# A gated mix of attention and expert lookup: the loads of the output stage in another order, all from SyncE

## The chip, the cores and the metric

The kernel runs on one core of a Trainium2 chip. Its time is the device time in microseconds. A profile is one execution taken by the hardware profiler: it has its own device time, and a span, which runs from the first instruction to the last. The engines are TensorE (PE in the profile, with PEld for its weight loads), VectorE (DVE), ScalarE (ACT), GpSimd (POOL) and SyncE (SP). Each works through its own instructions in order. A transfer is issued by SP, ACT or POOL and carried by 16 DMA engines that all of them share. The profile names the hardware queue of SP q1, that of ACT q10 and that of POOL q0.

## What is computed

Two branches share the input x of 2048 tokens by 1024 features, and a gate per token mixes them:

```python
g = _sigmoid((x * gate_w).sum(-1, keepdims=True))
a = _A_ref(x, A_wqkv, A_wo)      # 32 heads of 32, softmax attention, then @ wo
b = _B_ref(x, B_w_q, B_k1, B_k2, B_u, B_v)   # per token and head, one of 64 experts
return g * a + (1 - g) * b
```

Everything is float32. The attention branch ends in a product of the heads' outputs, 2048 x 1024, with `wo`, 1024 x 1024. The expert branch ends in a product of a 2048 x 64 matrix of weights with `v`. The output stage of the kernel makes both of these last products.

## The kernel before

The program has four parts: the projections with the routing of experts, the values, the attention over 32 heads, and the output stage. The change touches the last head of attention and the output stage, which begins at about 1644 us of the profile.

**What attention leaves in memory.** Each head writes its unnormalized output to `OD[g]` (od in the profile; `finish`, line 1378), where g is one of 8 groups of 4 heads, and its row sums to `SMD[g]` (smd; `norm_sums`, line 1385). When a group of four heads is done, `load_r` (line 1393) reads the four sums back (rr<-smd), and `norm_r` (line 1397) takes reciprocals on VectorE, multiplies by the gate, and stores them in `RD` (rd<-rr).

**Blocks.** The output stage works on 8 blocks of 256 tokens. For block n it needs the rows of all groups, `OC[n]` (tile V; `load_o`, line 1406: 8 loads of 128 KB, one per group), and the reciprocals spread over the 32 features of every head, `RB[n]` (tile rb for block 0, accd for the others; `load_rb`, line 1412: 4 loads of 256 KB for 8 groups, each of which reads the same rows of `RD` into 32 partitions). `load_chunk` (line 1419) calls both. The tiles V and accd have two buffers each, so that block n + 2 takes the place of block n.

**Precision.** Each operand is split into a high and a low part: ScalarE makes the high part by a copy, and VectorE the low part by a subtraction (`split`, line 93). A product is three products of parts.

**Blocks 0 and 1** are computed plainly: `split_o` (line 1589) scales the rows by the reciprocals and splits them, `wo_mm` (line 1517) multiplies by the split `wo` (woh and wol), `av_mm` (line 1527) adds the expert branch, and `plain_out` (line 1581) copies the four PSUM banks to the tile `post` (the memory of rb) and stores them (out<-rb). Block 0 and block 1 use the same four places of `post`, so that the copies of block 1 wait for the stores of block 0 to land:

```python
            nc.scalar.activation(post[:, i], ps, AF.Copy)
        else:
            nc.vector.tensor_copy(post[:, i], ps)
        store(n, j, half, post[:, i])
```

**Blocks 2 to 7** use seven products in place of eight (`unit`, line 1662, with `Halves`, which builds the sums of operands). Four products need combined weights T1 to T4, which the values part wrote to memory as TD, and which `load_t` (line 1561) loads: t0h and t0l into wo_raw for P5, t1h and t1l into wo_raw for P6, t2h and t2l into z and t3l for P7, t3h and t3l into halves of woh and wol for P4. Each is 1 MB. `scale_o` (line 1572) scales a block's rows on VectorE. In `unit(2)`, after product P1, stand in this order: the copies and stores of block 1 (`plain_out`), the operands S4 and A22, and the operands of block 3, whose first step is `scale_o(3)`; only then come the sums of P1, P6, P7 and P5 on VectorE that set their PSUM banks free. The banks go round: eight of them, four for block 0, four for block 1, then one for each product. P2 of `unit(2)` takes the bank that the first copy of block 1 sets free, and P7 of `unit(3)` needs a bank that those sums set free.

**What sets the order.** The program is written out in the order in which each engine works. During attention a table of steps (`at`, line 1445) says after which step of which head a load is issued; from the output stage on, the order of the calls is the order of the queues. SP issues each transfer when its buffer is free, and also waits then for the transfer eight places earlier to have landed, since the completion semaphores go round in eights.

Of the kernel before, what the change touches and what calls it, by code (L numbers as in the profile page):

```python
# [10 lines left out]
F32R = mybir.dt.float32r  # L11
# [7 lines left out]
H = 32  # L19
KC = D // 128  # L20
HC = KC // 2
NT = S // 128
NQ = S // 512
G = H // 4
W = 256
# [6 lines left out]
def gated_mha_peer_kernel(ctx, tc, xT, wqkv, wv, wo, wq, k12, ug, v, out):  # L32
# [8 lines left out]
    nc = tc.nc  # L41
# [32 lines left out]
    def dma(dst, src, queue=nc.sync):  # L74
        a, b = (ap.bitcast(F32) if ap.dtype == F32R else ap for ap in (dst, src))
        return queue.dma_start(a, b)  # L76
# [16 lines left out]
    def split(hi, lo, src, on=None):  # L93
        nc.scalar.activation(hi, src, AF.Copy)  # L94
        (on or nc.vector).tensor_tensor(out=lo, in0=src, in1=hi.bitcast(F32), op=OP.subtract)
# [13 lines left out]
    def bank():  # L109
        i = bank_no[0] % 8  # L110
        bank_no[0] += 1
        return ps1.tile([128, 512], F32, name=f"bk{i}")
# [788 lines left out]
    zp = Pool("zp", side="right")  # L901
# [357 lines left out]
    wk = Pool("wk", bufs=2)  # L1259
# [88 lines left out]
    def rowsum(ps, *srcs):  # L1348
        for src in srcs:
            for qc in range(NQ):  # L1350
                yield nc.tensor.matmul(ps[32 * qc:32 * qc + 32, :], ones,  # L1351
                                       src[:, qc * 512:(qc + 1) * 512],
                                       start=(src is srcs[0]), stop=(src is srcs[-1]))
# [52 lines left out]
    def load_o(n, k0, k1, queue=nc.sync):  # L1406
        if k0 == 0:
            OC[n] = vpool.tile([128, KC, W], F32, name="V")
        for kc in range(k0, k1):
            dma(OC[n][:, kc, :], OD[kc][:, n * W:(n + 1) * W], queue)  # L1410

    def load_rb(n, k0, k1, js=range(4), queue=nc.sync):
        if k0 == 0 and js[0] == 0:
            RB[n] = rb0 if n == 0 else wk.tile([128, KC, W], F32, name="accd")
        for j in js:
            src = RD[k0:k1, j:j + 1, n * W:(n + 1) * W].rearrange("g j s -> j g s")
            dma(RB[n][32 * j:32 * j + 32, k0:k1, :], src.to_broadcast([32, k1 - k0, W]), queue)
# [7 lines left out]
    OH, OL, W0 = {}, {}, []  # L1425
# [19 lines left out]
    def at(step, f, *a):  # L1445
        todo.setdefault(step, []).append((f, a))
# [25 lines left out]
    at(30 * NT + 13, load_rb, 0, 0, KC - 1, range(2))  # L1472
    at((H - 1) * NT + 2, load_rb, 0, 0, KC - 1, range(2, 4))
    at((H - 1) * NT + 8, load_rb, 1, 0, KC - 1)
    at((H - 1) * NT + 14, load_rb, 2, 0, KC - 1)


    BT = 2
# [34 lines left out]
    def load_at(n):  # L1513
        AT[n] = fin.tile([128, W], F32R, name="at", bufs=3)
        dma(AT[n], ATD[:, n * W:(n + 1) * W])
# [45 lines left out]
    def load_t(i, *parts):  # L1561

        ops = ht.b.setdefault(f"T{i + 1}", [None, None])
        for n, (part, src) in enumerate(zip(parts, TD[i])):
            if part is None:
                continue
            m = HC // len(part)
            for j, place in enumerate(part):
                dma(place, src[:, m * j:m * j + m, :].rearrange("p k m -> p (k m)"))
            ops[n] = [place[:, k * 512:(k + 1) * 512] for place in part for k in range(m)]  # L1570
# [18 lines left out]
    def split_o(n, k0, k1):  # L1589
        o = OC[n][:, k0:k1, :]  # L1590
        nc.vector.tensor_mul(o, o, RB[n][:, k0:k1, :])
        split(OH[n][:, k0:k1, :], OL[n][:, k0:k1, :], o)

    def banks4():
        return {(i, half): bank() for i in range(W // 128) for half in range(2)}
# [4 lines left out]
    finish(H - 1)  # L1600
    sm = pso.tile([128, 512], F32, name="o")
    list(rowsum(sm, *(P[H - 1, NT - i] for i in (1, 2)), ACC.pop(H - 1)))
    load_o(1, 0, KC - 1, nc.gpsimd)
    split_hi(1)
    for kc in range(1, KC - 1):
        split_hi(kc + 1)
        if kc == 1:
            norm_sums(H - 1, sm, nc.scalar)
            load_r(G - 1)
            for n in range(2):  # L1610
                load_at(n)
            pso.close()
        split_lo(kc)
        wo_mm(pa, 0, [kc], False, False)
    norm_r(G - 1)
    for n in range(2):
        load_chunk(n, KC - 1, KC)
    load_rb(2, KC - 1, KC)
    split_lo(KC - 1)
    split(woh[0], wol[0], raw_wo(0))  # L1620

    load_t(2, None, [fin.tile([128, S], F32R, name="t3l")])
    load_t(0, *([keep.tile([128, S], F32R, name=f"wo_raw{j}")] for j in range(2)))
    ps_odd = Pool("ps_odd", space=PSUM)
    for (i, half), ps in pa.items():
        av_mm(0, i, half, ps)
    split_o(0, KC - 1, KC)
    wo_mm(pa, 0, [KC - 1], False, True)  # L1630
    OH[1] = zp.tile([128, KC, W], F32R, name="z1")
    OL[1] = wk.tile([128, KC, W], F32R, name="acc")
    for k0, k1 in ((0, HC), (HC, KC)):
        split_o(1, k0, k1)
    load_o(2, 0, KC)
    load_at(2)
    load_t(2, [zp.tile([128, S], F32R, name="z0")], None)
    load_t(1, *([keep.tile([128, S], F32R, name=f"wo_raw{2 + j}")] for j in range(2)))
    pa1 = banks4()
    wo_mm(pa1, 1, list(range(KC - 1)), True, False)  # L1640
    for (i, half), ps in pa1.items():
        av_mm(1, i, half, ps)
    plain_out(0, pa)
    load_t(3, *([part[k][:, 512:] for k in range(HC)] for part in (woh, wol)))
    load_rb(3, 0, KC, queue=nc.scalar)
    load_o(3, 0, KC)
    ht.places(wk.tile([128, S], F32R, name="acc"), "A11", "A12")
    ht.places(fin.tile([128, S], F32R, name="s31"), "S3", "S1")
    scale_o(2)
# [121 lines left out]
```

## Time and profile before

| | us |
|---|---|
| median of three runs | 1827.84 |
| the three runs | 1827.28, 1827.84, 1831.94 |
| the profiled execution's own time | 1832.25 |
| its span | 1830.4 |
| what lies around the span | 1.85 |
| PE busy in the span | 1817.8 |

The page of the profile gives the busy time of each engine and the costliest groups of instructions. Below it, the trace answers questions about single instructions: a timeline of one engine, in which a bracket at the end of a row tells how long the engine had been idle and what ended that; busy time, granted TensorE clock and DMA rate in chosen stretches; and the chain of work that ended last. Matmul rows are pipelined: of two rows that follow one another, the second's start counts, not the first's end.

### The profile page before, as it was taken

The numbers are of one execution on the slowest core, as the hardware profiler recorded it, in microseconds if no ns is written. First come the engines' busy times: TensorE is split into PE (matmuls) and PEld (weight loads), VectorE is DVE, ScalarE is ACT, GpSimd is POOL, SyncE is SP. The second block draws the span as 40 slices with busy tenths as digits, with TensorE's granted clock in tenths as the row PEclk, the third lists the DMA queues.
The fourth block names the chain that finished last, engine by engine and source line by source line (L and its number), as shares of the span: only waits on it lengthen the run. The fifth ranks groups of instructions, "written<-read, shape, count | busy, mean of one in ns | idle before, by whom it ended". The sixth has DMA issues, their size and how long they took to land.

```text
span 1830.4 us, 26559 instructions
## 1 busy us (share of the span) xinstructions
PE 1817.8 (99%) x10083; PEld 1099.8 (60%) x10083; DVE 1461.4 (80%) x1258; ACT 1312.5 (72%) x1716; POOL 231.7 (13%) x358
## 2 busy tenths in 40 slices
PE   9999999999999999999999999999999999999999
PEld 6777777788888644444444444444444444447787
DVE  7866876789967888888888888888888888884675
ACT  5545544522433699999999999999999999992221
POOL 1222222244001100000000000000000000010000
PEclk9999999999999999999999999999999999999999
DMA  7888689660267777776777777777777777776872
GB/s 271 277 277 280 209 296 286 199 215 9 83 240 247 219 157 178 158 177 154 177 176 164 186 165 182 171 173 167 174 186 159 178 159 182 174 138 180 281 164 78
DMA packets 127441, 345.24 MB, mean 189 GB/s; under 512 B 17168, under 2 KB 57904, under 8 KB 107920
## 3 DMA queue, kind: packets, MB, share of 16 engines
q1 hardware_dynamic: 95688, 193.40, 36.0%
q0 software_dynamic: 28224, 145.92, 34.1%
q10 hardware_dynamic: 3400, 4.20, 1.0%
q8 instruction: 80, 1.31, 0.3%
q14 instruction: 49, 0.40, 0.1%
HBM read 171.76 MB, written 72.36 MB: 133 GB/s over the span
## 4 chain that ended last, share of the span: by engine, by line
PE 88%; DMA 5%; issue 3%; DVE 1%; ACT 1%; SPq 1%; POOL 1%; DVEq 0%; ACTq 0%; POOLq 0%
PE ring L1317 28%; PE o L1338 25%; PE bk L302 15%; PE pa L963 5%; PE bk L724 5%; PE bk L982 2%; PE bk L290 2%; PE bk L341 2%; PE ring L1351 1%; PE bk L963 1%; SPq L76 1%; DMA accd<-rd 1%; DMA accd<-P 1%; DMA smd<-ssb 1%; DMA z<-t2h 1%
## 5 line engine op out<-in xcount | busy, mean ns | idle before, releaser
L1327 ACT ACTIVATE P<-ring 128x1024 f32<-128x1024 f32 (+2 forms) x1031 | 912.7, 983 | 14.5 <-DMA accd<-P 1.9
L1367 DVE TENSOR_TENSOR acc<-acc,P 128x2048 f32<-128x2048 f32 x319 | 730.9, 2291 | 72.6 <-ACT P L1327 47.1
L1338 PE MATMUL o<-P,V 128*32 128x512 f32 x3840 | 464.8, 599 | 0.0
L1317 PE MATMUL ring<-Q,K 98*128 98x512 f32 x1024 | 272.2, 407 | 0.4 <-ACT P L1327 0.3
L1317 PE MATMUL ring<-z,z 98*128 98x512 f32 x1020 | 270.6, 407 | 0.6 <-ACT accd L1327 0.6
L1317 PEld LDWEIGHTS ring<-Q,K 98*128 98x128 f32 x1024 | 182.0, 188 | 144.8 <-ACT P L1327 73.8
L1317 PEld LDWEIGHTS ring<-z,z 98*128 98x128 f32 x1020 | 181.3, 188 | 142.8 <-ACT P L1327 72.0
L1338 PEld LDWEIGHTS o<-P,V 128*32 128x32 f32 x3840 | 98.8, 109 | 223.1 <-issue 214.5
L1360 POOL DMA_DIRECT2D accd<-P x95 | 81.5, 858 | 931.5 <-ACT P L1327 406.5
L1365 DVE TENSOR_TENSOR acc<-P,P 128x2048 f32<-128x2048 f32 x32 | 73.4, 2293 | 74.8 <-ACT P L1327 74.8
L302 PE MATMUL bk<-xh,A 128*128 128x512 f32 x336 | 82.8, 396 | 0.0
L302 PE MATMUL bk<-xh,S 128*128 128x512 f32 x336 | 81.3, 393 | 0.0
L302 PE MATMUL bk<-xl,S 128*128 128x512 f32 x336 | 80.1, 391 | 0.0
L135 ACT ACTIVATE hi<-u 128x512 fp32r<-128x512 f32 x42 | 26.5, 632 | 70.0 <-issue 39.4
L302 PEld LDWEIGHTS bk<-xh,A 128*128 128x128 f32 x336 | 62.1, 188 | 23.8 <-issue 5.0
L1370 DVE TENSOR_TENSOR acc<-acc,accd 128x2048 f32<-128x2048 f32 x32 | 73.1, 2284 | 0.0
L302 PEld LDWEIGHTS bk<-xl,S 128*128 128x128 f32 x336 | 62.8, 188 | 16.3 <-issue 2.5
L302 PEld LDWEIGHTS bk<-xh,S 128*128 128x128 f32 x336 | 62.4, 188 | 14.5 <-issue 1.7
L1327 ACT ACTIVATE accd<-ring 128x1024 f32<-128x1024 f32 (+2 forms) x64 | 62.2, 1032 | 2.3 <-PE ring L1317 2.2
L963 PE MATMUL pa<-woh,acc 128*128 128x512 f32 x192 | 62.2, 389 | 0.0
L511 DVE TENSOR_TENSOR u<-u,bk 128x512 f32<-128x512 f32 x70 | 46.6, 682 | 10.0 <-DMA wpd<-u 5.8
L94 ACT ACTIVATE acc<-V 128x512 fp32r<-128x512 f32 x24 | 14.5, 625 | 50.8 <-DVE V L1576 14.4
(302 smaller groups left out, 2204.9 us busy)
## 6 DMA issues: line engine op xcount, KB each, us to landing
accd<-P POOLq DMA_DIRECT2D x95, 1024.0 KB, 7.6
wqt<-in_wq SPq DMA_DIRECT2D x64, 512.0 KB
wraw<-in_wqkv SPq DMA_DIRECT2D x28, 512.0 KB
kdh<-hi POOLq DMA_DIRECT2D x32, 256.0 KB, 5.3
kdl<-lo POOLq DMA_DIRECT2D x32, 256.0 KB, 6.5
qdh<-hi POOLq DMA_DIRECT2D x32, 256.0 KB, 5.9
qdl<-lo POOLq DMA_DIRECT2D x32, 256.0 KB, 5.9
z<-kdh SPq DMA_DIRECT2D x32, 256.0 KB
```

What stands on the lines that cost most here:

```text
L290: nc.tensor.matmul(b0[w, n], AW[PLAIN[w, ki]][a][:, k, :], X[f"B{ki + 1}{n + 1}"][b][:, k, :], start=first, stop=last)
L302: nc.tensor.matmul(ps, a[i][:, k, :], b[j][:, k, :], start=(k == 0 and i == j == 0), stop=(k == HC - 1 and i == 1))
L511: nc.vector.tensor_tensor(out=out, in0=a, in1=b, op=OP.add)
L724: nc.tensor.matmul(ps, x_part(a, t // 4, kc)[:, tok], b, start=first, stop=last)
L963: nc.tensor.matmul(ps, self.a[a][i][:, k, :], self.b[b][j][k], start=(not first and k == 0 and i == j == 0), stop=(k == HC - 1 and i == 1))
L1317: on_ring(nc.tensor.matmul(ring[:, i, :], K[:98, kt * 128:(kt + 1) * 128], Q[:98, qc * 512:(qc + 1) * 512], start=True, stop=True), i)
L1327: on_ring(nc.scalar.activation(P[h, kt][:, q0 * 512:(q0 + m) * 512].rearrange("p (a m) -> p a m", a=m), ring[:, i:i + m, :], AF.Exp, scale ...
L1338: nc.tensor.matmul(O[h][32 * qc:32 * qc + 32, :], Vt[g][:, kt, 32 * j:32 * j + 32], p[:, qc * 512:(qc + 1) * 512], start=(kt == 0), stop=( ...
L1360: nc.gpsimd.dma_start(ACCD[h], P[h, kt], accum_op=OP.add)
L1365: nc.vector.tensor_add(ACC[h], P[h, 0], P[h, kt])
L1367: nc.vector.tensor_add(ACC[h], ACC[h], P[h, kt])
L1370: nc.vector.tensor_add(ACC[h], ACC[h], ACCD[h])
```

## The change

The loads of the output stage are issued in another order, and all of them from SyncE:

- The reciprocals of block 2 (`load_rb(2, ...)`) are no longer loaded during the last head for seven groups with the eighth later, but whole, after the small loads that follow `norm_r`.
- The rows of block 1 (`load_o(1, 0, 7)`) move from the queue of GpSimd, right after the last head, to that of SyncE, behind `load_r` and the two loads of expert weights.
- The rows of block 2 go out ahead of the combined weights T1.
- The reciprocals and rows of block 3 (`load_rb(3)`, `load_o(3)`) go out ahead of the stores of block 0 and of T4. The reciprocals were on the queue of ScalarE behind `plain_out(0)`, the rows on that of SyncE behind T4.
- `split_o(1, 0, 4)`, the first half of block 1, is worked off ahead of `split_o(0, 7, 8)`, the last group of block 0, on VectorE and ScalarE.

No instruction is added or removed but for the four DMAs that loaded the eighth group of block 2's reciprocals apart.

```diff
     at((H - 1) * NT + 8, load_rb, 1, 0, KC - 1)
-    at((H - 1) * NT + 14, load_rb, 2, 0, KC - 1)
...
     list(rowsum(sm, *(P[H - 1, NT - i] for i in (1, 2)), ACC.pop(H - 1)))
-    load_o(1, 0, KC - 1, nc.gpsimd)
     split_hi(1)
...
             for n in range(2):
                 load_at(n)
+            load_o(1, 0, KC - 1)
             pso.close()
...
     for n in range(2):
         load_chunk(n, KC - 1, KC)
-    load_rb(2, KC - 1, KC)
+    load_rb(2, 0, KC)
     split_lo(KC - 1)
     split(woh[0], wol[0], raw_wo(0))
     load_t(2, None, [fin.tile([128, S], F32R, name="t3l")])
+    OH[1] = zp.tile([128, KC, W], F32R, name="z1")
+    OL[1] = wk.tile([128, KC, W], F32R, name="acc")
+    split_o(1, 0, HC)
+    split_o(0, KC - 1, KC)
+    load_o(2, 0, KC)
     load_t(0, *([keep.tile([128, S], F32R, name=f"wo_raw{j}")] for j in range(2)))
     ps_odd = Pool("ps_odd", space=PSUM)
     for (i, half), ps in pa.items():
         av_mm(0, i, half, ps)
-    split_o(0, KC - 1, KC)
     wo_mm(pa, 0, [KC - 1], False, True)
-    OH[1] = zp.tile([128, KC, W], F32R, name="z1")
-    OL[1] = wk.tile([128, KC, W], F32R, name="acc")
-    for k0, k1 in ((0, HC), (HC, KC)):
-        split_o(1, k0, k1)
-    load_o(2, 0, KC)
+    split_o(1, HC, KC)
     load_at(2)
     load_t(2, [zp.tile([128, S], F32R, name="z0")], None)
     load_t(1, *([keep.tile([128, S], F32R, name=f"wo_raw{2 + j}")] for j in range(2)))
+    load_rb(3, 0, KC)
+    load_o(3, 0, KC)
...
     plain_out(0, pa)
     load_t(3, *([part[k][:, 512:] for k in range(HC)] for part in (woh, wol)))
-    load_rb(3, 0, KC, queue=nc.scalar)
-    load_o(3, 0, KC)
```

The first place is the queue of SP from the last head's sums on. In these rows od_71 to od_77 are the rows of the first seven groups and od_78 those of the eighth; accd<-rd are reciprocals of blocks 1 and 2. Before:

```order
L76 DMA accd<-rd 32x7x256 x8
L76 DMA od_78<-osb 4x32x512
L76 DMA rr<-smd_87 128x64
L76 DMA at<-atd 128x256 x2
L76 DMA rd<-rr 128x64
L76 DMA V<-od_78 128x256
L76 DMA rb_5505<-rd 32x256 x4
L76 DMA V<-od_78 128x256
L76 DMA accd<-rd 32x256 x8
L76 DMA t3l<-t2l 128x2048
```

And in the changed kernel:

```order
L76 DMA accd<-rd 32x7x256 x4
L76 DMA od_78<-osb 4x32x512
L76 DMA rr<-smd_87 128x64
L76 DMA at<-atd 128x256 x2
L76 DMA V<-od_71 128x256
...
L76 DMA V<-od_77 128x256
L76 DMA rd<-rr 128x64
L76 DMA V<-od_78 128x256
L76 DMA rb_5505<-rd 32x256 x4
L76 DMA V<-od_78 128x256
L76 DMA accd<-rd 32x256 x4
L76 DMA accd<-rd 32x8x256 x4
L76 DMA t3l<-t2l 128x2048
```

Four large loads of reciprocals have left the place ahead of the last head's store and stand ahead of t3l, and seven loads of rows stand between the sums' load and the store of the reciprocals.

The second place is the queue of SP around the stores of block 0 (the first `out<-rb`). Before:

```order
L76 DMA wo_raw_12668<-t1l 128x2048
L76 DMA out<-rb_5505 128x512 x4
L76 DMA woh_12439<-t3h 128x512
...
L76 DMA wol_12434<-t3l 128x512
L76 DMA V<-od_71 128x256
...
L76 DMA V<-od_78 128x256
L76 DMA at<-atd 128x256
```

And in the changed kernel:

```order
L76 DMA wo_raw_12664<-t1l 128x2048
L76 DMA accd<-rd 32x8x256 x4
L76 DMA V<-od_71 128x256
...
L76 DMA V<-od_78 128x256
L76 DMA out<-rb_5505 128x512 x4
L76 DMA woh_12434<-t3h 128x512
...
L76 DMA wol_12429<-t3l 128x512
L76 DMA at<-atd 128x256
```

The stores of block 0 now stand behind 12 loads for block 3, four of reciprocals and eight of rows.

The third place is VectorE after the last split of `wo`, where V<-V,rb with L95 behind it is the last group of block 0, and V<-V,accd a half of block 1. Before:

```order
L1591 TENSOR_TENSOR V<-V,rb_5505 128x256
L95 TENSOR_TENSOR acc<-V,z_12285 128x256
L1591 TENSOR_TENSOR V<-V,accd 128x1024
L95 TENSOR_TENSOR acc<-V,z_12646 128x1024
L1591 TENSOR_TENSOR V<-V,accd 128x1024
```

And in the changed kernel:

```order
L1590 TENSOR_TENSOR V<-V,accd 128x1024
L95 TENSOR_TENSOR acc<-V,z_12612 128x1024
L1590 TENSOR_TENSOR V<-V,rb_5505 128x256
L95 TENSOR_TENSOR acc<-V,z_12285 128x256
L1590 TENSOR_TENSOR V<-V,accd 128x1024
```

The first half of block 1 has moved ahead of the last group of block 0.

## The prediction

> **What bounds the kernel now.** I read the page first, then the stretches of the output stage, then the timelines of PE, SP, DVE and ACT there. The page:
>
> ```profile
> span 1830.4 us, 26559 instructions
> PE 1817.8 (99%) x10083; PEld 1099.8 (60%) x10083; DVE 1461.4 (80%) x1258; ACT 1312.5 (72%) x1716; POOL 231.7 (13%) x358
> ```
>
> PE is the bound: only 12.6 us of the span are without a matmul. An order of loads can win only what PE idles in the stage that it touches, and lose whatever it makes PE idle more. The timeline of PE shows the gaps there (a row's bracket is the idle time ahead of it):
>
> ```profile
> 1669.27 1.20 PE L1522 MATMUL pa<-woh,z 128*128 128x512 f32 x4 [1.39 <-ACT z L94]
> 1694.81 1.07 PE L1522 MATMUL pa<-woh,acc 128*128 128x512 f32 x4
> 1699.36 0.47 PE L963 MATMUL pa<-z,s 128*128 128x512 f32 x1 [0.76 <-ACT osb L1678]
> 1707.62 0.62 PE L1529 MATMUL pa<-vhl,at 128*128 128x512 f32 x2
> 1722.73 0.67 PE L963 MATMUL pa<-z,s 128*128 128x512 f32 x1 [2.26 <-DVE rb L969]
> ```
>
> The first gap is ahead of the last group of block 0, the second ahead of P7 of unit 2, the third ahead of P7 of unit 3. The two rows without a gap are the last matmuls of block 1 and, at 1707.62, the place where P2 of unit 2 begins. After the last gap the granted clock falls to a half, which the stretch right behind it shows (its seventh figure group is PEclk, then the DMA share and GB/s):
>
> ```profile
> 1722.83:1726.24 3.41, 3.41 (x9) 2.67 (x10) 2.63 (x5) 1.15 (x2) 0.00 (x0) 0.50 0.74 88
> ```
>
> 3.41 us at half clock cost 1.7 us. So the stage holds 1.39 + 0.76 + 2.26 + 1.7 = 6.1 us that better order could win, 0.33% of the time, and no more.
>
> The other limit in the stage is the transfers. These stretches show the rates: twice weights, then rows, then a broadcast of reciprocals alone:
>
> ```profile
> 1672.50:1679.00 6.50, 6.50 (x31) 5.36 (x30) 4.22 (x5) 2.03 (x3) 0.00 (x0) 1.00 0.96 382
> 1697.00:1701.00 4.00, 3.24 (x15) 2.39 (x14) 2.56 (x5) 2.27 (x4) 0.00 (x0) 1.00 1.01 424
> 1711.00:1714.00 3.00, 3.00 (x15) 2.47 (x14) 0.55 (x1) 0.00 (x0) 0.00 (x0) 1.00 0.99 340
> 1759.00:1769.00 10.00, 10.00 (x46) 8.29 (x45) 8.37 (x14) 2.79 (x5) 0.00 (x0) 1.00 0.55 89
> ```
>
> Weights move at 382 to 424 GB/s and rows at 340, but the broadcast at 89: a `load_rb` of 1.05 MB takes four times as long as the same bytes of weights. Every load that is moved must be weighed by this. SP's timeline, and below it ACT's and DVE's:
>
> ```profile
> 1660.98 0.85 SPq L76 DMA_DIRECT2D at<-atd  x2
> 1667.41 3.67 SPq L76 DMA_DIRECT2D accd<-rd  x8
> 1671.18 0.37 SPq L76 DMA_DIRECT2D t3l<-t2l  x1
> 1691.54 1.70 SPq L76 DMA_DIRECT2D wo_raw<-t1l  x1
> 1693.67 2.60 SPq L76 DMA_DIRECT2D out<-rb  x4
> 1707.50 4.78 SPq L76 DMA_DIRECT2D V<-od  x8
> ```
>
> ```profile
> 1670.85 1.06 ACT L94 ACTIVATE z<-V 128x1024 fp32r<-128x1024 f32 x1 [1.63 <-DVE V L1591]
> 1678.51 11.14 ACTq L76 DMA_DIRECT2D accd<-rd  x2
> 1705.51 0.60 ACT L1584 ACTIVATE rb<-pa 128x512 f32<-128x512 f32 x1 [4.52 <-DMA out<-rb]
> ```
>
> ```profile
> 1668.34 0.43 DVE L1591 TENSOR_TENSOR V<-V,rb 128x256 f32<-128x256 f32 x1 [2.40 <-DMA rb<-rd]
> 1669.59 1.22 DVE L1591 TENSOR_TENSOR V<-V,accd 128x1024 f32<-128x1024 f32 x1
> 1704.88 0.69 DVE L1586 COPY rb<-pa 128x512 f32<-128x512 f32 x1 [3.16 <-PE pa L963]
> 1706.18 0.69 DVE L1586 COPY rb<-pa 128x512 f32<-128x512 f32 x1 [0.61 <-DMA out<-rb]
> 1708.17 1.29 DVE L95 TENSOR_TENSOR acc<-V,acc 128x512 fp32r<-128x512 f32 x2 [0.70 <-ACT acc L94]
> 1713.45 1.23 DVE L1576 TENSOR_TENSOR V<-V,accd 128x1024 f32<-128x1024 f32 x1 [3.99 <-DMA V<-od]
> 1715.29 1.22 DVE L1576 TENSOR_TENSOR V<-V,accd 128x1024 f32<-128x1024 f32 x1 [0.61 <-DMA V<-od]
> 1721.18 0.68 DVE L969 TENSOR_TENSOR rb<-osb,pa 128x512 f32<-128x512 f32 x1
> ```
>
> Here is the hinge. The copies of block 1 start at 1704.88, 1705.51 and 1706.18, 0.65 us apart: they follow the stores of block 0 as these land (the first row names PE, but block 1's last matmuls started at 1694.81, 10 us before). The stores were issued at 1693.67 and landed 11 us later, since the queue ahead was full. The first copy frees the bank of P2 at 1705.57; PE comes there at 1707.62, 2.0 us later. That is all the slack the stores of block 0 have, and the change puts 12 loads ahead of them.
>
> **The change part by part.**
>
> *Block 3's rows earlier (a gain).* In the rows above VectorE waits 3.99 us for block 3's rows (1713.45), so the sums that free PE's banks come at 1721.18, and P7 of unit 3 waits 2.26 us. With the rows ahead of the stores they land before the copies begin. Gain 2.26, and the clock's 1.7 there.
>
> *The early loads (a gain).* The chain of waits, and DVE's wait for the sums:
>
> ```profile
> 1650.21 10.26 DMA smd<-ssb
> 1660.54 2.29 DMA rr<-smd
> 1663.70 1.46 DMA rd<-rr
> ```
>
> ```profile
> 1658.78 0.42 DVE L1556 TENSOR_TENSOR acc<-V,z 128x256 fp32r<-128x256 f32 x1
> 1662.86 0.55 DVE L1399 RECIPROCAL rr<-rr 128x64 f32<-128x64 f32 x1 [3.67 <-DMA rr<-smd]
> ```
>
> And what had been issued by then, from the list of issues between 1640 and 1664:
>
> ```profile
> V<-od POOLq DMA_DIRECT2D x7, 128.0 KB, 11.5
> accd<-rd SPq DMA_DIRECT2D x4, 224.0 KB
> ```
>
> The 8 KB of sums took 10.26 us to land, the next 32 KB 2.29: at 1650 the queues held 0.9 MB of block 1's rows and 0.9 MB of block 2's reciprocals. Both leave this place, so I price the store between 2.3 and 10.26 and take 2.3, like its neighbour. Then SP issues rr at 1652.6, the two at loads (0.85) and the seven loads of rows (at most 0.6 each, by the row of 1707.50) by 1658; DVE is free for the reciprocal at 1659.2, 3.67 earlier than now, and everything behind it moves by that much. Between rd<-rr (1663.70 now, 1660.0 then) and t3l (1671.18) SP has 7.5 us of issues, of which four small ones (half of the 3.67) fall away: the first load of block 2's reciprocals is issued at 1660.0 + 7.5 - 1.9 = 1665.6. On DVE and ACT the first half of block 1 (1.22 on DVE, 1.06 on ACT, 1.22 on DVE, with 0.1 at each handover) now precedes the last group of block 0: it can begin when the last splits of `wo` are done, at 1662.4, and ends at 1666.0; that group follows (0.43 + 0.42) at 1667.0, still ahead of 1667.88, where PE asks for it. The 1.39 us gap closes with 0.9 us to spare. Its cover is the early sums: without them the gap would be some 4 us longer.
>
> *P7 of unit 2 (a gain).* It waits 0.76 for T3's high part. Ahead of that load stand the same megabytes as now with one broadcast for the other, begun 5.6 us earlier. Gain 0.76. P5, P6 and `scale_o(2)` gain slack likewise and are priced at nothing.
>
> *The stores of block 0 (the loss).* I compare with the run as it was, from the first issue of the backlog to the first copy. Before: t3l issued 1671.18, copy 1704.88, that is 33.7 us. After: the backlog begins at 1665.6, 5.6 earlier, and has one broadcast and one set of rows more ahead of the stores. Rows: 1.05 MB at 340 GB/s, 3.1 us. The broadcast: 11.8 at 89 GB/s from the row of a stretch where it runs alone. Where it ran from ACT's queue beside SP's, the queue's row over 36 us gives the engine time:
>
> ```profile
> q10 hardware_dynamic: 1088, 1.05, 24.8%
> ```
>
> 24.8% of 36 us is 8.9, the low end if others filled every gap. A third reading comes from the 33.7 us: six weights (6.3 MB at 400, between 382 and 424 in stretches of weights, 15.7), rows with the expert weights (1.18 MB, 3.5), the first store (0.7) and one small transfer's latency (2.3) leave 11.5 for block 3's broadcast, although it came from another queue. I take 11.0, nearest to the two readings that agree.
> The move of block 3's broadcast from ACT's queue to SP's is priced at nothing, since it already took its full share there; had ACT's queue hidden it, the 33.7 us would have been some 22.
>
> First store landed: 1704.9 + 11.0 + 3.1 - 5.6 = 1713.4. The copy (0.69) and the release (0.14) let PE start P2 at 1714.2 instead of 1707.62: 6.6 later. PE gets there at 1707.62 - 1.39 - 0.76 = 1705.5, so it will idle 8.7 us where there was no gap.
>
> *What is late next.* S4 and A22 follow the copies as now. VectorE ends A22 4.6 us after the first copy begins (1704.88 to 1709.46), at 1718.0; `scale_o(3)` takes 2.4 without a wait; P7 can start 6.2 after that (1715.29 + 1.22 = 1716.5 to 1722.73), at 1726.6. PE needs the bank 12.8 us after P2's start (1707.62 to 1720.47) plus the clock's loss, at 1728.7 or later. No gap. T4's loads follow the stores in the same distance as now.
>
> *The clock.* A gap of 2.26 already halved it for 3.41 us; one of 8.7 does so at least as long: 1.7, at most twice that; I take 2.2.
>
> *POOL* loses seven issues that PE never waited for; ACT loses four, the last two of which held it for 11.14 us while nothing that PE needed stood behind them. Nothing.
>
> Sum at P7 of unit 3: +6.6 - 2.26 (gap gone) - 1.7 + 2.2 (clock) = **+4.8 us**. Later units keep their distances, since block 4's loads follow the copies as before. Profiled: 1832.25 + 4.8 = 1837.1.
>
> This execution stands 4.4 above the median 1827.84; one of the three runs (1831.94) stands as high, the other two lower by about the size of the gap of unit 3 with its clock (4.0). If the short runs lack that gap, the change has that much less to gain there. I put the forecast between 1837.1 and 1837.1 - 4.4, at **1835**.
>
> **The rivals.**
>
> *A: the sums stay slow.* If the store of the sums still takes 10.26 us, the rows of block 1 lie between rr and rd: SP issues rd at about 1665.5, the backlog begins at 1671.1, 5.5 later, and P2 as much: 1842.6 profiled, 1838 to 1843. For it: the sums' store was ACT's only transfer in its queue and still took 10.26. Against: 1.8 MB were in flight, and small transfers without that took 2.3.
> The Trainium skill, "DMA: Bandwidth & Descriptors", section "Queues, rings and completion order", has each DMA engine go round between queues packet by packet. By that rule a backlog on SP and POOL could not hold up ACT's store for long, so the change would not shorten it; the 10.26 beside 2.29 speaks against the rule here, and no run yet separates the two.
>
> *B: faster.* If block 2's broadcast overlaps with the weights behind it, so that it and block 3's rows together cost no more than 5.3 us (the earlier start of 5.6 less 0.3), the first store lands by 1704.6, PE never waits at P2, and the three gaps and the clock loss go: -6.1, 1826.1 profiled, 1822 on the median. For it: the broadcast alone fills only 0.55 of the DMA engines. Against: even at 8.9 it and the rows take 12.0.
>
> *C: the same mechanism, smaller.* With the broadcast at 8.9 and a clock loss of 1.7 the shift is 2.2: 1830 to 1834.
>
> **How the numbers follow.** 0.3% is 5.5 us, about what a measurement can tell from no change (the three runs spread over 4.7). Forecast 0.65, A 0.15, C 0.14, B 0.06. Slower by over 0.3% means over 1833.3: two thirds of the forecast (0.44), all of A, a little of C: 0.60. Faster means under 1822.4, which only B reaches and barely: 0.03. The rest, 0.37, is the same. The range from 1829 to 1843 takes in C and A and leaves out B and the tails.
>
> **What would show it.** In the profile after: a gap of 6 to 13 us ahead of unit 2's `av_mm` (vhl,at), released by a copy of pa to rb, with the copies waiting for out<-rb; clock at a half behind it; no gap at P7 of unit 3; the sums landed in under 4 us; no gap at the last group of block 0. Wrong would be: copies beginning by 1706, sums still at 10 us, or a gap elsewhere, at P4 for T4 or at unit 4 for its reciprocals.

## The result and the profile after

The changed kernel takes 1839.8 us (median of 8 runs, 1837.9 to 1842.2); the kernel before, run beside it, takes 1831.3 (8 runs, 1827.3 to 1836.6). The ratio is 1.0049, with a 95% interval from 1.0035 to 1.0063: slower by 0.5%. The profiled execution took 1839.4 us. The first lines of its page:

```profile
span 1837.6 us, 26539 instructions
PE 1817.9 (99%) x10083; PEld 1099.3 (60%) x10083; DVE 1461.4 (80%) x1258; ACT 1312.5 (71%) x1716; POOL 227.5 (12%) x351
```

PE is busy for as long as before (1817.9 beside 1817.8) in a span that is 7.2 us longer. All that was lost is idle time of PE. Its timeline in the output stage shows where (the bracket is the idle time ahead of a row):

```profile
1697.84 0.39 PE L963 MATMUL pa<-z,s 128*128 128x512 f32 x1
1704.37 2.79 PE L963 MATMUL pa<-wo_raw,z 128*128 128x512 f32 x11 [0.69 <-DMA wo_raw<-t1l]
1717.33 1.22 PE L1528 MATMUL pa<-vhl,at 128*128 128x512 f32 x2 [10.18 <-DVE rb L1585]
1732.04 0.39 PE L963 MATMUL pa<-z,s 128*128 128x512 f32 x1
```

The gaps at P7 of unit 2 (1697.84) and at P7 of unit 3 (1732.04) are gone, and so is the one ahead of the last group of block 0. In their place stand 10.18 us ahead of P2 of unit 2, with 0.69 before it, at the low part of T2 (t1l). The clock around the large gap, in two stretches (granted clock, DMA share and GB/s stand last):

```profile
1711.10:1717.33 6.23, 0.00 (x1) 0.01 (x1) 0.69 (x1) 0.11 (x1) 0.00 (x0) 0.50 0.85 293
1717.33:1721.34 4.01, 4.01 (x10) 3.14 (x11) 2.33 (x4) 2.12 (x4) 0.00 (x0) 0.50 0.90 295
```

It fell to a half while PE stood idle, which costs nothing, and stayed there for 4.01 us of work, which cost 2.0. The chain of work that ended last runs through the transfers here:

```profile
1651.32 1.15 DMA smd<-ssb
...
1671.14 13.52 DMA V<-od
1685.13 8.02 DMA wo_raw<-t0l
1693.16 20.08 DMA accd<-rd
1713.68 2.81 DMA out<-rb
```

SP's own timeline gives the order of the issues, and how long the queue held each group up:

```profile
1653.08 0.34 SPq L76 DMA_DIRECT2D rr<-smd  x1
1661.00 0.32 SPq L76 DMA_DIRECT2D rd<-rr  x1
1664.73 3.79 SPq L76 DMA_DIRECT2D accd<-rd  x8
1671.14 13.47 SPq L76 DMA_DIRECT2D V<-od  x8
1688.90 4.63 SPq L76 DMA_DIRECT2D accd<-rd  x4
1694.71 18.87 SPq L76 DMA_DIRECT2D V<-od  x8
1713.68 1.86 SPq L76 DMA_DIRECT2D out<-rb  x4
```

The stores of block 0, issued at 1693.67 before, are issued at 1713.68: SP needs 18.87 us to put block 3's eight loads of rows into a full queue. It issues the last of them only when the transfer eight places earlier, block 3's last broadcast, has landed: that is the chain's row of 20.08 us from 1693.16 on. VectorE shows both ends of it:

```profile
1660.16 0.55 DVE L1399 RECIPROCAL rr<-rr 128x64 f32<-128x64 f32 x1
1716.58 0.69 DVE L1585 COPY rb<-pa 128x512 f32<-128x512 f32 x1 [16.69 <-DMA out<-rb]
1718.21 0.69 DVE L1585 COPY rb<-pa 128x512 f32<-128x512 f32 x1 [0.94 <-DMA out<-rb]
1721.51 2.35 DVE L1575 TENSOR_TENSOR V<-V,accd 128x1024 f32<-128x1024 f32 x2
```

The reciprocal no longer waits for the sums, and block 3's rows are there when `scale_o(3)` asks (1721.51, no bracket). The copies of block 1 pay for both: the first waits 16.69 us for a store of block 0 and starts at 1716.58, where it started at 1704.88.

The sum of the idle time closes. I measure the stage from the last `o` matmuls of the attention; this row is that of the kernel before, the next that of the changed one:

```profile
1640.22 3.64 PE L1338 MATMUL o<-P,V 128*32 128x512 f32 x32
```

```profile
1641.32 3.64 PE L1338 MATMUL o<-P,V 128*32 128x512 f32 x32
```

The stage took 1830.4 - 1640.22 = 190.2 us before and 1837.6 - 1641.32 = 196.3 after, 6.1 more: 10.87 of gaps for 4.41, less 0.4 in the tail behind the last matmul. The other 1.1 us lay ahead of the stage already. The executions differ there by as much without the change: in the runs below that keep the attention as it is the row stands between 1640.5 and 1641.6, and at 1641.5 in one with the loads in the attention ordered as before.

### The profile page after: what moved, and what is told of

It is laid out like the page before. It is cut to its first block, busy times and chain, and to the rows that moved or that the text cites. A ratio compares the mean times of both kernels' runs of the same rounds, so it can differ in the third digit from the quotient of the medians.

```text
span 1837.6 us, 26539 instructions
## 1 busy us (share of the span) xinstructions
PE 1817.9 (99%) x10083; PEld 1099.3 (60%) x10083; DVE 1461.4 (80%) x1258; ACT 1312.5 (71%) x1716; POOL 227.5 (12%) x351
## 4 chain that ended last, share of the span: by engine, by line
PE 90%; DMA 4%; issue 3%; DVE 2%; POOL 1%; ACT 1%; SPq 0%; DVEq 0%; POOLq 0%; ACTq 0%
PE ring L1317 28%; PE o L1338 26%; PE bk L302 15%; PE pa L963 6%; PE bk L724 5%; PE bk L982 2%; PE bk L290 2%; PE bk L963 2%; PE bk L341 2%; PE ring L1351 1%; DMA accd<-rd 1%; DMA V<-od 1%; PE pa L1528 1%; DMA wo_raw<-t0l 0%; PE bk L190 0%
## 5 line engine op out<-in xcount | busy, mean ns | idle before, releaser
L1338 PE MATMUL o<-P,V 128*32 128x512 f32 x3840 | 464.8, 599 | 0.0
```

The lines of the kernel that those rows point to most:

```text
L1338: nc.tensor.matmul(O[h][32 * qc:32 * qc + 32, :], Vt[g][:, kt, 32 * j:32 * j + 32], p[:, qc * 512:(qc + 1) * 512], start=(kt == 0), stop=( ...
```

## The experiments

Where a single run is given, there is no interval. The kernel before, measured beside these runs, had medians between 1830.3 and 1831.4.

**Stores first.** Block 3's loads go behind the stores of block 0, the rest of the change stays (against the changed kernel):

```diff
-    load_rb(3, 0, KC)
-    load_o(3, 0, KC)
     pa1 = banks4()
...
     plain_out(0, pa)
+    load_rb(3, 0, KC)
+    load_o(3, 0, KC)
     load_t(3, *([part[k][:, 512:] for k in range(HC)] for part in (woh, wol)))
```

> The changed kernel with the loads of block 3 (reciprocals and rows) put back behind the stores of block 0, still ahead of T4, all on SP. My theory (the transfers of this stretch are worked off in the order of the queue at a fixed price each, and PE waits for whichever it needs first): the first copy of block 1 comes 14 us earlier than the 1716.6 of the changed kernel, at 1702 to 1705, and the gap of 10.2 us at P2 of unit 2 is gone; but T4 and block 3's rows still land at 1718 to 1724, so that a gap of 5 to 9 us opens at P4 of unit 2. Time 1834 to 1839, between the two kernels. Rival (the stores' place alone is the fault, the queue has room): no gap over 3 us anywhere behind 1700 and a time at or under that of the kernel before.

Measured: 1838.5 us, a single run. VectorE's first copy, and then PE's gaps in unit 2:

```profile
1701.65 0.69 DVE L1585 COPY rb<-pa 128x512 f32<-128x512 f32 x1 [2.61 <-DMA out<-rb]
```

```profile
1718.98 0.77 PE L963 MATMUL pa<-woh,acc 128*128 128x512 f32 x1 [6.41 <-DMA woh<-t3h]
1723.06 0.79 PE L963 MATMUL pa<-wol,acc 128*128 128x512 f32 x1 [3.31 <-DMA wol<-t3l]
```

The copy comes 14.9 us earlier and the gap ahead of P2 is gone, but T4's loads, now behind block 3's, open gaps of 6.41 and 3.31, 9.7 in sum for the one gap of 5 to 9 that was expected. Here the order decided only who waits.

**Block 3's reciprocals on ACT's queue** (against the changed kernel):

```diff
-    load_rb(3, 0, KC)
     load_o(3, 0, KC)
...
     plain_out(0, pa)
+    load_rb(3, 0, KC, queue=nc.scalar)
```

> The changed kernel with the reciprocals of block 3 alone put back on ScalarE's queue behind the copies of block 0. My theory (a broadcast takes its share of the DMA engines whichever queue issues it): first copy of block 1 within 3 us of the changed kernel's 1716.6, gap at P2 of 7 to 10 us, time 1836 to 1841. Rival (ScalarE's queue runs beside SP's and hides it): first copy by 1708, gap under 2 us, time about 1831.

Measured: 1837.2 us, a single run. VectorE's first copy and PE's largest gap:

```profile
1715.12 0.69 DVE L1585 COPY rb<-pa 128x512 f32<-128x512 f32 x1 [9.55 <-DMA out<-rb]
```

```profile
1706.86 0.47 PE L963 MATMUL pa<-z,s 128*128 128x512 f32 x1 [3.23 <-DMA z<-t2h]
```

With the broadcast of block 3 no longer in their queue the stores land only 1.5 us earlier: it delays them from the other queue nearly as much. The place of the gaps was expected wrongly. ACT issues the broadcast early, T3's weights and block 2's rows suffer instead, and PE loses 2.74 us at P1 and 3.23 at P7 of unit 2 and has no gap at P2.

**Block 2's reciprocals early again** (against the changed kernel): seven of eight groups are loaded in the last head, as before the change.

```diff
+    at((H - 1) * NT + 14, load_rb, 2, 0, KC - 1)
...
-    load_rb(2, 0, KC)
+    load_rb(2, KC - 1, KC)
```

> The changed kernel with seven groups of block 2's reciprocals loaded in the last head again, as before, and the eighth later. My theory: the backlog ahead of the stores is 11 us shorter, first copy of block 1 at 1704 to 1707, gap at P2 under 2 us, no gap at P7 of unit 3. The sums' store has 0.9 MB of reciprocals ahead of it again: it takes 5 to 10 us instead of 1.2, and as the rows of block 1 stand behind it, the last group of block 0 comes late, a gap of 2 to 6 us there. Time 1828 to 1834. Rival (a queue's backlog cannot hold up another queue's store, since the DMA engines go round between queues): the sums' store takes under 3 us, no early gap, time 1825 to 1829.

Measured: 1832.3 us (10 runs), ratio 1.0007 to the kernel before, interval 0.9998 to 1.0017. The chain, SP's issue of t3l, the first copy, and PE's gaps:

```profile
1650.59 8.05 DMA smd<-ssb
```

```profile
1671.72 0.37 SPq L76 DMA_DIRECT2D t3l<-t2l  x1
```

```profile
1708.41 0.69 DVE L1586 COPY rb<-pa 128x512 f32<-128x512 f32 x1 [5.44 <-DMA out<-rb]
```

```profile
1670.17 1.39 PE L1522 MATMUL pa<-woh,z 128*128 128x512 f32 x4 [1.90 <-ACT z L94]
1744.41 0.47 PE L963 MATMUL pa<-z,s 128*128 128x512 f32 x1 [1.32 <-DVE rb L969]
```

Taking this one broadcast out of the backlog takes the loss away. From t3l to the first copy it is 36.7 us, within 0.1 the 33.7 of before and 3.1 for the rows that the prediction has; the copy itself came 1.4 us behind the latest time that was expected. The early gap is back at 1.90, P7 of unit 4 has one of 1.32, and the sums take 8.05 us to land although POOL has no load of rows here. So a broadcast in SP's queue, with no load on POOL's, holds ACT's 8 KB store for 8 us. By the rule that rival A drew from the Trainium skill ("DMA: Bandwidth & Descriptors", "Queues, rings and completion order") SP's backlog would not do so; the 8.05 us decide against that reading here.

**Block 1's rows on POOL again** (against the changed kernel):

```diff
+    load_o(1, 0, KC - 1, nc.gpsimd)
...
-            load_o(1, 0, KC - 1)
```

> The changed kernel with the rows of block 1 put back on GpSimd's queue right after the last head; no reciprocals of block 2 beside them. My theory (what is in flight holds up the sums' store, whatever its queue): the store takes 3 to 7 us, against 1.2 without and 10.3 with both. Rival (only SP's own broadcast holds it up): under 2 us. Either way the stores of block 0 do not move by more than 2 us, and the time stays at 1837 to 1841.

Measured: 1840.4 us, a single run; PE waits 9.77 us at P2 and the first copy comes at 1717.28. The sums' store is issued at 1651.52 in this run, and SP can issue the next step here:

```profile
1654.96 0.34 SPq L76 DMA_DIRECT2D rr<-smd  x1
```

That is 3.4 us behind the store, where it is 1.8 in the changed kernel (1651.32 to 1653.08). The rows beside the store cost 1.6 us, the broadcast 6.3 (8.1 in the run above less 1.8). Behind the rows alone the first copy comes only 0.7 us later than in the changed kernel, as was expected.

**Only block 3's rows first** (against the kernel before):

```diff
+    load_o(3, 0, KC)
     load_t(3, *([part[k][:, 512:] for k in range(HC)] for part in (woh, wol)))
...
-    load_o(3, 0, KC)
```

> The kernel before with one part of the change alone: the rows of block 3 are loaded ahead of T4 instead of behind it. My theory: they land 5 us earlier, about 1708, before VectorE comes to them at 1709.5, so that the gap of 2.3 us at P7 of unit 3 and the half clock behind it go; T4 lands 3 us later, at 1714 to 1716, which P4 of unit 2 meets without a gap over 1 us. Time 2 to 4 us under the kernel before. Rival (T4 has no slack): a gap of 2 to 4 us at P4, no gain.

Measured: 1831.0 us (10 runs), ratio 1.0002, interval 0.9992 to 1.0012. The expected gain isn't there, though the gap at P7 of unit 3 is gone. PE and VectorE in unit 4:

```profile
1742.45 0.47 PE L963 MATMUL pa<-z,s 128*128 128x512 f32 x1 [1.87 <-DVE rb L969]
```

```profile
1733.87 2.36 DVE L1576 TENSOR_TENSOR V<-V,accd 128x1024 f32<-128x1024 f32 x2 [6.19 <-DMA accd<-rd]
```

The gap has moved one unit on, where block 4's reciprocals are now what comes last: a broadcast is late there, not rows. This does not explain the time in full. In the profiled execution, one of the faster ones (1829.5), the stage takes 1827.7 - 1641.55 = 186.2 us, 4.0 less than in the profile of the kernel before, while the ten runs show no gain. So one execution's stage can lie some us from the usual one, and why is open.

**The broadcasts over two queues** (against the changed kernel): two heads of each group on SP, two on ACT.

```diff
-    load_rb(2, 0, KC)
+    load_rb(2, 0, KC, range(2))
...
+    load_rb(2, 0, KC, range(2, 4), nc.scalar)
...
-    load_rb(3, 0, KC)
+    load_rb(3, 0, KC, range(2))
...
+    load_rb(3, 0, KC, range(2, 4), nc.scalar)
```

> The changed kernel with each load of reciprocals of blocks 2 and 3 split: the first two heads of every group on SP, the last two on ScalarE's queue, at about the same time. Theory D (the broadcast is slow because each of its transfers writes 32 partitions only, and two of them side by side write 64): the two loads together take 9 to 12 us less, first copy of block 1 at 1704 to 1708, gap at P2 under 2.5 us, time 1828 to 1832. Theory S (it is slow because all 32 partitions read the same rows of memory, or costs its engine time in any case): first copy within 4 us of 1716.6, time 1835 to 1841.

Measured: 1835.7 us (8 runs), ratio 1.0030, interval 1.0019 to 1.0040. PE at P2:

```profile
1713.51 1.22 PE L1528 MATMUL pa<-vhl,at 128*128 128x512 f32 x2 [4.88 <-DVE rb L1585]
```

By the numbers this is theory S (within 4 us, 1835 to 1841), but at its edge: the gap is half as long, the first copy 3.8 us earlier (1712.76), and the early gap is open again at 2.34. A queue of its own helps a broadcast somewhat, but doesn't hide it.

**Other rows** (against the changed kernel): for blocks 2 and 3 each of the 128 partitions reads a row of its own, from the input; the same number of rows of the same length arrive. The values of blocks 2 and 3 of the output are therefore not the reference's.

```diff
         for j in js:
+            if n in (2, 3):
+                rows = xT.rearrange("(g j p) s -> j p g s", g=KC, j=4)[j]
+                dma(RB[n][32 * j:32 * j + 32, k0:k1, :], rows[:, k0:k1, n * W:(n + 1) * W], queue)
+                continue
```

> The changed kernel, but blocks 2 and 3 take as their reciprocals 32 different rows of the input for each transfer instead of one row 32 times, in the same shapes, places and order, so that what these blocks give is not the reference's. Theory S (the same rows read 32 times are slow): each load takes 3 to 5 us instead of 11, the stores of block 0 land 12 to 15 us earlier, no gap at P2, time 1827 to 1831. Theory D (32 partitions at the receiving end are slow): still 10 to 12 us each, gap at P2 of 9 to 11 us, time 1837 to 1841.

Measured: 1828.6 us, a single run. The issue on SP, VectorE's first scale of block 2 and its first copy of block 1, and PE at P2:

```profile
1666.78 1.81 SPq L76 DMA_DIRECT2D accd<-in_xT  x4
```

```profile
1677.85 1.23 DVE L1579 TENSOR_TENSOR V<-V,accd 128x1024 f32<-128x1024 f32 x1 [4.86 <-DMA V<-od]
1705.95 0.69 DVE L1589 COPY rb<-pa 128x512 f32<-128x512 f32 x1 [6.01 <-DMA out<-rb]
```

```profile
1706.70 0.73 PE L1532 MATMUL pa<-vhl,at 128*128 128x512 f32 x2 [0.47 <-DVE rb L1589]
```

From the issue to the first scale it is 11.1 us, where the changed kernel needs 19.1 (1666.6, half way through the row of 1664.73, to 1685.70); the copy comes 10.6 us earlier (12 to 15 were expected) and the gap at P2 shrinks to 0.47. So it isn't the 32 receiving partitions that make the broadcast slow. Reading the same rows 32 times is one reading of that, the memory they lie in another; the next runs separate them.

**Copies in memory.** Each group's reciprocals are written 32 times, one copy for each partition that reads them, by one transfer of 1 MB within memory during the attention; blocks 2 and on read 128 different rows. The last group stays a broadcast. The same edit stands in the changed kernel, in the kernel before, and in the kernel before with block 3's rows first:

```diff
+    RC = dram.tile([G - 1, 128, S], F32, name="rc")
...
+    def copy_r(g):
+        src = RD[g:g + 1].rearrange("g j s -> j g s").to_broadcast([4, 32, S])
+        dma(RC[g].rearrange("(j q) s -> j q s", j=4), src)
...
+        if n >= 2 and k0 == 0:
+            src = RC[:, :, n * W:(n + 1) * W].rearrange("g p s -> p g s")
+            dma(RB[n][:, :G - 1, :], src, queue)
+            k0 = G - 1
-        for j in js:
+        for j in js if k0 < k1 else ():
...
+            at(base + 2 * NT + 4, copy_r, g)
```

> The changed kernel, with the reciprocals of groups 0 to 6 written 32 times, once for each row that receives them, by one copy in memory per group during the attention (line copy_r), so that blocks 2 and on read rows that are all different; the last group's reciprocals are still read 32 times from one row. Theory S (a broadcast is slow because the same rows are read 32 times, run e7_other_rows): block 2's reciprocals take 5 to 6 us where they took 11, the first copy of plain_out(0) comes 1706 to 1708, the gap ahead of P2 of unit 2 is 0 to 1, block 4's reciprocals come in time, so that unit 4 has no gap at P7 (run e7_other_rows had one of 1.42 there), and the time is 1826 to 1829. Rival T (run e7_other_rows was fast because its rows were read from the input, in another place of memory): the loads stay at 11 us, the gap ahead of P2 at about 10, the time at 1839 to 1840. A third way: the seven copies of 1 MB collide with the attention's own transfers, PE gets gaps before 1640, and the time is above 1832 although the output stage is as theory S says.

> The same copies in the kernel before, order of loads unchanged. Theory S: the early gap of 1.39 ahead of the last group of block 0 is as it was or smaller; block 3's reciprocals, on ACT's queue behind plain_out(0), land 5 us earlier, so the gap of 2.26 ahead of P7 of unit 3 and the half clock behind it are gone, nothing is late at P7 of unit 4, and the time is 1826 to 1828. Rival T: no change, 1830 to 1831. Third way: above 1832, with gaps before 1640.

> The same copies in the kernel before with block 3's rows loaded ahead of load_t(3) (run e5_rows3_first, which gained nothing because the gap of unit 3 came back in unit 4, where block 4's reciprocals were late). Theory S: with short reciprocals nothing is late in unit 4 either, so e5's gain is now kept: 1825.5 to 1828, equal to the kernel before with copies within 1 us. Rival T: 1830 to 1831 as in run e5_rows3_first.

Measured: 1852.6, 1853.4 and 1853.8 us, ratios 1.0125 (1.0108 to 1.0142), 1.0122 (1.0105 to 1.0139) and 1.0128 (1.0111 to 1.0145). As to the time, the third way came true in the first two; the expectation of the third run had no such way, and both of its times were wrong. As to the output stage, theory S did: PE has no gap there in any of the three. The last block's reciprocals, alone in the queues, show the price. First a stretch of the changed kernel while they arrive, then one of the first run with copies:

```profile
1790.00:1792.00 2.00, 2.00 (x11) 1.65 (x10) 1.22 (x3) 0.73 (x2) 0.00 (x0) 1.00 0.54 88
1792.00:1794.00 2.00, 2.00 (x11) 1.65 (x10) 2.00 (x4) 0.42 (x1) 0.00 (x0) 1.00 0.56 78
```

```profile
1793.00:1795.00 2.00, 2.00 (x11) 1.65 (x10) 0.64 (x1) 0.00 (x0) 0.00 (x0) 1.00 1.01 349
```

Into the same partitions, in runs of the same length: 78 to 88 GB/s from one row for 32 readers, 349 from a row for each. (The fast load moves seven groups in one transfer, not eight in four; in the run with other rows four transfers were fast too.) The copies lie in scratch memory of the kernel like the single rows, not in the input, so rival T falls.

The loss is in the attention. The run's last `o` matmuls, and the group of the score matmuls with its idle time:

```profile
1667.73 3.64 PE L1339 MATMUL o<-P,V 128*32 128x512 f32 x32
```

```profile
L1318 PE MATMUL ring<-z,z 98*128 98x512 f32 x1020 | 275.4, 410 | 16.8 <-ACT P L1328 16.1 <-ACT accd L1328 0.6
```

The stage begins 26.4 us later than in the changed kernel and then takes 1850.8 - 1667.73 = 183.1 us, 13.2 less. In the attention POOL adds tiles of P into accd by transfers of 1 MB. In the changed kernel and then in the run with copies, at the same place of a head (in the second, SP issues a copy at 917.82):

```profile
926.92 0.86 POOL L1360 DMA_DIRECT2D accd<-P  x1 [13.71 <-ACT P L1327]
934.73 0.86 POOL L1360 DMA_DIRECT2D accd<-P  x1 [6.95 <-ACT P L1327]
```

```profile
929.31 0.86 POOL L1361 DMA_DIRECT2D accd<-P  x1 [14.05 <-DMA accd<-P]
942.42 0.86 POOL L1361 DMA_DIRECT2D accd<-P  x1 [12.25 <-DMA accd<-P]
```

Beside the copy POOL waits for the transfer before it, which it doesn't at this place of the changed kernel; P's buffers come free late, ACT waits (22.6 us over the run for these transfers, 0.8 in the changed kernel), then PE. Idle time accounts for 16.8 of the 26.4 us (0.6 without the copies); the rest is longer busy time of PE (470.4 us in the `o` matmuls, 464.8 without the copies), with a mean granted clock of 0.995 over the run.

How the copies were written has a part in this. At this place PE waits 3.17 us, and in that time the DMA engines are busy for only a quarter (the figure before the last of the second row):

```profile
942.62 0.61 PE L1318 MATMUL ring<-z,z 98*128 98x512 f32 x1 [3.17 <-ACT P L1328]
939.00:941.00 2.00, 0.44 (x2) 0.01 (x1) 1.90 (x2) 0.00 (x0) 0.00 (x0) 1.00 0.23 70
```

The trace records the completion of a copy in four parts, 23.7 to 25.8 us after its issue at 917.82, where an accumulating transfer completes in sixteen. Of the one issued at 929.31 twelve parts are done within 6.9 us and four only at 11.8 to 12.6. I read this as copies, whose outer dimension is the four heads, that keep four of the sixteen DMA engines busy and hold up what else these have to carry. A copy spread over all sixteen was not tried. Each copy also reads its rows 32 times, and yet between 926 and 942 its packets of 8 KB took 0.31 to 0.32 us, like those of the combined weights (0.31 between 1674 and 1678 of the profile before). So reading a row again and again need not be slow; whether the broadcast is slow because all sixteen engines read the same rows at once was not tested.

**The copies in pieces.** The same with six pieces of 128 KB a group, spread over two heads:

```diff
-    def copy_r(g):
-        src = RD[g:g + 1].rearrange("g j s -> j g s").to_broadcast([4, 32, S])
-        dma(RC[g].rearrange("(j q) s -> j q s", j=4), src)
+    def copy_r(g, n):
+        c = slice(n * W, (n + 1) * W)
+        src = RD[g:g + 1, :, c].rearrange("g j s -> j g s").to_broadcast([4, 32, W])
+        dma(RC[g][:, c].rearrange("(j q) s -> j q s", j=4), src)
...
-            at(base + 2 * NT + 4, copy_r, g)
+            for n, step in zip(range(2, S // W), (5, 10, 14, 21, 26, 30)):
+                at(base + 2 * NT + step, copy_r, g, n)
```

> As run e8_copies_after, but the copy of each group's reciprocals is cut into six pieces of 128 KB (256 columns each, those of blocks 2 to 7), spread over two heads of the attention, since in run e8_copies_after the copies of 1 MB delayed the accumulating transfer of the sums (accd from P) on which ACT's P waits and cost 16.8 us of gaps on PE in the attention, while the output stage had no gap at all. If the size of the copy was what cost: no gap above 1 us in the attention, none in the output stage, and the time is that of the kernel before less its gaps (1.39, 0.76, 2.26) and the half clock (1.7): 1824 to 1827. Rival: any copy in the attention delays the accumulating transfers by what it moves: the gaps stay near 16 us in sum and the time is 1845 to 1852.

> The same pieces in the kernel before, order of loads unchanged. If the size of the copy was what cost: 1824 to 1827, within 1.5 us of run e11_pieces_after, that is, with short loads of the reciprocals the two orders come out alike. Rival: 1845 to 1852. A third way: the order of before is better by over 2 us, since its block 2 has all but the last group's reciprocals in place before the stage.

Measured: 1848.1 us in the changed kernel, ratio 1.0095 (1.0079 to 1.0111), and 1847.0 in the kernel before, 1.0097 (1.0082 to 1.0112). The score matmuls of the first:

```profile
L1318 PE MATMUL ring<-Q,K 98*128 98x512 f32 x1024 | 276.3, 409 | 7.4 <-ACT P L1328 7.2
L1318 PE MATMUL ring<-z,z 98*128 98x512 f32 x1020 | 274.3, 409 | 5.4 <-ACT P L1328 4.7 <-ACT accd L1328 0.6
```

12.8 us of idle time in many small waits for 16.8 in a few large: the rival holds in the main. But the pieces, too, complete in four parts, and beside one the accumulating transfer issued at 927.03 has twelve parts done within 7.0 us and the last four at 10.0 to 11.1. So what is shown is that the attention has no room for copies of this form. The output stage again has no gap, and takes 1846.3 - 1663.41 = 182.9 and 1842.7 - 1659.59 = 183.1 us (the second number of each is the start of the last `o` matmuls). The stage in one table, each row from one profiled execution:

| kernel | stage, us |
|---|---|
| before | 190.2 |
| changed | 196.3 |
| changed, block 2's reciprocals early again | 188.8 |
| before, block 3's rows first | 186.2 |
| changed, other rows for blocks 2 and 3 | 185.4 |
| copies: changed / before / before with rows first | 183.1 / 183.4 / 183.4 |
| copies in pieces: changed / before | 182.9 / 183.1 |

With short loads of the reciprocals the two orders come out alike, 7 us below the kernel before. No version that beats it as a whole was found, since the copies cost the attention more; copies made elsewhere, or spread over all the DMA engines, were not tried.

## Why the prediction was right and where it was off

The side, the place and the mechanism were right: the stores of block 0 behind 12 loads, the copies behind the stores, PE idle at P2. By its own steps:

*The early loads.* Right. The sums' next step comes 1.8 us behind their store (2.3 taken), the reciprocal runs at 1660.16 without a wait, the first half of block 1 precedes the last group of block 0, and no gap is left there. Rival A is false for this kernel. Its reason was tested by bringing the broadcast back (8.05 us) and the rows back (3.4 us): the broadcast was the larger cause.

*Block 3's rows earlier* and *P7 of unit 2.* Both gaps closed. But a gap of 0.69 opened behind P7 of unit 2, at T2's low part, a load that stands in the same backlog; the prediction gave the products behind P7 only a gain in slack. It cost nothing more, since PE would have idled as much longer at P2.

*The stores of block 0.* The step that was off. The first copy was put at 1713.4 and came at 1716.58, 3.2 later. 1.1 of it was there before the stage began. The rest is the size of the backlog: from the first issue of block 2's reciprocals to the copy 47.8 us were predicted (33.7 + 11.0 + 3.1), and 50.0 passed (1666.6 to 1716.58). With block 2's reciprocals out of it (run "early again") it was 36.7, so the rows were sized rightly, and the mis-sized term is the broadcast in the backlog: 13.3 us (50.0 - 36.7) in place of 11.0. Both readings that gave 11.0 were of broadcasts in other places. PE idled 10.18 + 0.69 us for the predicted 8.7.

*What is late next.* Right: no gap at P7 of unit 3, none for T4 and none behind.

*The clock.* Right in size: 2.0 lost (2.2 taken, the bounds 1.7 and 3.4). The larger gap did not make the half clock's working part much longer, 4.01 us for 3.41.

*POOL and ACT at nothing* holds; so does the move of block 3's broadcast to SP at nothing, within the 1.5 us that the run on ACT's queue shows.

*The sum* was +4.8, and the stage grew by 6.1: the gaps came out 2.2 longer (10.87 for 8.7), 0.4 of it came back in the tail, and PE's busy time, with the half clock in it, grew by 0.1 for the 0.5 that were taken. Rival C, which made the broadcast cheaper, lay on the wrong side; rival B needed it to overlap with the weights, and even two queues hid only part of it.

*From the sum to the time.* The profiled sum was 1837.1, the profiled time 1839.4. The forecast then went down to 1835, half way to the median of three runs, on the thought that short runs of the kernel before lack a gap. Over 8 runs that median was 1831.3, close to the profiled 1832.25, and the changed kernel's, 1839.8, is close to its profile too. This step down was the largest part of the miss, 2.1 of 4.8 us; the stage gave 1.3, 1.1 lay ahead of it, and the median is 0.4 above the profiled time. Between the two medians lie 8.5 us, between the two profiled executions 7.2, and the stage accounts for 6.1; the rest is not explained by the change.

## What to carry to other kernels

Weigh a moved load by the time that it holds the queues, not by its bytes: here a broadcast of 1 MB was worth 13 us of backlog, and rows of the same size 3. When a gap closes and the time stays, look one unit further for the load that is late there; most of these gaps came from one slow form of load, and no order of the issues that was tried cured it. Before blaming traffic as such, see over how many DMA engines a transfer is spread. A median of three runs is a weak ground for leaving the profile's own sum.

## What the runs showed that I had not expected

Reading one row of memory for 32 partitions ran at 78 to 88 GB/s, reading a row for each at 349, in pieces of equal length. An 8 KB store from ACT's queue took 8 us beside a broadcast in SP's, 3.4 beside rows in POOL's, and under 2 without either. And the attention, with DMA engines busy for only about three quarters of the time (0.75 to 0.76 in the stretches between 800 and 1600), could not take copies of even 128 KB that complete in four parts without PE waiting: four parts of the accumulating transfer beside one came 3 to 4 us behind the other twelve, and POOL waits for one such transfer before it issues the next.
